# Sharing the first sequence's products with the decays between VectorE and GpSimd

## The chip, the cores and the metric

The kernel runs on one core of one Trainium2 chip. The metric is the device time of one execution in microseconds (us), the median of several runs. The core's engines are named as the profile names them: PE (TensorE, matmuls; PEld is its weight load), DVE (VectorE), ACT (ScalarE), POOL (GpSimd), and SP, which here only issues transfers. A row of the profile that ends in q (SPq, ACTq) is the issuing of a transfer.

## The reference, cut to what matters

Four sequences of 768 tokens and 8 heads go through a state-space recurrence in chunks; the result, 3072 tokens of 256 values, goes through a two-layer network with a tanh GELU between the layers.

```python
# attention-like part, for each batch and head, chunk by chunk
cum = np.cumsum(log(clip(a, 1e-6, 1)))
M = einsum('bhin,bhjn->bhij', C, B) * exp(cum_i - cum_j) * causal
y = einsum('bhij,bhjd->bhid', M, x) + einsum('bhin,bhnd->bhid', C, state) * exp(cum)
state = exp(cum_last) * state + sum_j B_j x_j exp(cum_last - cum_j)
# network
h = y.reshape(3072, 256) @ w_in            # 256 -> 2048
out = gelu_tanh(h) @ w_out                 # 2048 -> 256
```

The kernel does not form the matrix of decays. It multiplies B by a running product of decays and C by that product's reciprocal, so that the product of the two carries the ratio. These are "the products of B and C with the decays".

## The kernel before, in words

The 3072 tokens are 24 chunks of 128. The chunks are grouped in 13 units: chunk 0, chunk 1, then pairs. Sequence 0 holds the units 0 to 3 (two of one chunk, two pairs), and its preparation is written apart from that of the others, since everything waits for it.

Preparation of sequence 0. Four small loads bring the decays `a`; DVE clips them (`f_clip`, L505), forms the running product from the back (`f_R`, L509) and transposes it (`f_RT`, L513). B and C of sequence 0 arrive as 128 partitions of 6 tokens x 8 heads x 16 values. `f_mul(0)` multiplies B by the decays and `f_mul(1)` multiplies C by their reciprocal (`f_recip`, L516); both stand at L593, each is one DVE instruction over 768 elements a partition. `f_pe` (L578, L579) and the matmul `f_pp` with `f_pend` make the decay over a whole chunk. PE transposes B's product (`f_T(0,0)`, six matmuls, one for each of the six tokens, into the bank yb) and C's (`f_T(1,0)` and `f_T(1,1)`, three tokens each, into two banks hp). `f_E` copies B's bank to `bh`, and `f_F` copies C's banks to `ce` with a mask for even and one for odd heads: for each of the two banks, each of the two masks, and two stretches of columns (0 to 43, which holds the first two chunks, and 43 to 128, the rest), eight instructions. In the kernel before bank 0's first stretch is copied by ACT and bank 1's by DVE. `f_N` and `f_bn` make B's untransposed copy.

Per unit. `f_G` (L683) forms C times B in the four banks gb, `f_M` (L693) masks it causally on DVE, `f_D` (L704) forms the chunk's part of the state, `f_S` and `f_SP` (L753, L760) carry the state on DVE, `f_Y` (L726, L735) sums the output in bank yb, and `f_yev` evicts it to `xm`. From unit 4 on, `f_YDG(u)` issues Y of unit u, D and G of unit u+1 in one run. The network follows: `f_s1(u, i)` (L780) is one step of the first layer into a bank hp (there are two such banks), `f_gelu` (L788) evicts it on ACT, `f_s2(u, chunk, quarter)` (L800) adds a quarter of the second layer into o_ps or yb, `f_oev` evicts it and `f_store` stores it. `f_s1(0, i)` and `f_s1(1, i)` need the quarter i of the first weight, `f_s2(.., q)` the quarter q of the second. These weights arrive as fp32 on SP's queue during the first 23 us, and are cast to bf16 by `f_wi` (quarter, half) and `f_wo` (quarter, half), on whichever of POOL, ACT and DVE the table says. `f_castx` casts x.

Sequences 1 to 3 are prepared by other functions, all on DVE: `f_clipg`, `f_scang`, `f_rT`, `f_qT`, `f_mulg` (L552), `f_Tg` (a 32x32 transpose, L562) and `f_Fg` (the masks, L572). `f_bq` copies B's product for the `f_bn` loads.

What sets the order. Every instruction group is a node with an engine, a duration that the author estimated, its dependences and a priority. `run_order` (L39) plays the nodes through once when the kernel is built and takes, on the engine that is free first, the ready node of lowest priority; on DVE and POOL it may also leave the engine idle for a node that is due soon. The order so found is what each engine executes; the chip follows it with semaphores, engine by engine, in order. The table `PRIO` (L96 to L258) overrides the priority of every node, and `ENG` (L260) the engine of some. Where the plan has PE idle before the first step of the second layer, `idle` (L1141) puts matmuls on zeros (L1149) in its place; there are 102.

Nodes take and free buffers: two banks hp, one bank yb, one o_ps, one set gb, six o_sb.

Of the kernel before, what the change touches and what calls it, by code (L numbers as in the profile page):

```python
# [31 lines left out]
def run_order(nodes, pools, hop=0.08, same=0.04, idle=None, wait=()):  # L32
# [64 lines left out]
    'load_x(0,)': 4, 'f_par()': -99.836, 'f_hq()': -99.485, 'load_wi(0,)': 5, 'f_pari()': -101.601,  # L97
    'f_clip()': -101.591, 'load_x(1,)': 6, 'f_R()': -4.443, 'f_selq()': -64.105, 'f_RT()': -101.591,
# [172 lines left out]
def kernel(  # L271
# [10 lines left out]
    nc = tc.nc  # L282

    batch, H, S, D = x.shape
# [902 lines left out]
```

## Time and profile before

| what | value |
|---|---|
| three runs | 116.16, 115.05, 116.52 us; median 116.16 |
| the profiled execution's own time | 116.01 us |
| its span in the trace | 114.3 us (1.71 us lie around it) |
| granted PE clock | 1.00 in every stretch |
| PE busy | 108.3 us, 95% |
| DVE, ACT, POOL busy | 73.6, 72.2, 19.3 us |
| PE busy from 0 to 12.32 us (mostly matmuls on zeros) | 10.18 us |
| PE busy from 12.32 to 20 us | 7.12 of 7.68 us |
| PE busy from 20 to 30.25 us | 9.73 of 10.25 us |
| PE busy from 30.25 to 112 us | 81.26 of 81.75 us |
| DMA engines' busy share in those four stretches | 0.88, 1.08, 0.93, 0.39 |

Times in the text are counted from the start of the span. A row of the timeline gives the start, the busy time, engine, line, operation, output and inputs with their shapes, and how often it came; in brackets is how long the engine had been idle before and what ended that. Matmuls overlap: four of 256 columns take a slot of 0.44 us in the chain although their row shows 0.60.

### The profile page before, as it was taken

To read this page: it belongs to the slowest core of one execution; us is meant where nothing else is said; L and a number is where in the kernel's file an instruction comes from. 1 tells how busy PE (TensorE), PEld (TensorE's weight loads), DVE (VectorE), ACT (ScalarE), POOL (GpSimd) and SP (SyncE) were. 2 spreads that over 40 slices of the span, in tenths; PEclk is the share of its full clock that TensorE was granted. 3 is DMA by queue.
4 is the path that set the end of the run, shared out by engine and by line. 5 is a ranking of instruction groups with operands and counts; after the bars stand their busy time and mean duration, and the time that the engine had idled before them with its cause. 6 is when DMAs were issued, how large, how long until landed. Compare 5 with 4: busy or idle time off the path is not lost.

```text
span 114.3 us, 3546 instructions
## 1 busy us (share of the span) xinstructions
PE 108.3 (95%) x1466; PEld 95.7 (84%) x1466; DVE 73.6 (64%) x168; ACT 72.2 (63%) x137; POOL 19.3 (17%) x45
## 2 busy tenths in 40 slices
PE   5989898999899999999999999999999999999990
PEld 5967784988687989998988899979898889999990
DVE  5799859857997899975959899336592940000111
ACT  0537885678485467667766767675776666777710
POOL 6725536623202001202000200004000000000000
PEclk9999999999999999999999999999999999999999
DMA  1999999899376487386677102573101110111021
GB/s 44 259 325 321 380 308 256 256 206 158 103 154 120 119 192 156 101 164 125 148 186 157 51 2 69 125 148 53 49 9 46 52 46 0 46 52 46 16 73 49
DMA packets 44268, 14.77 MB, mean 129 GB/s; under 512 B 39004, under 2 KB 42716, under 8 KB 44252
## 3 DMA queue, kind: packets, MB, share of 16 engines
q1 hardware_dynamic: 43100, 14.10, 51.1%
q10 hardware_dynamic: 1152, 0.45, 1.5%
q8 instruction: 11, 0.18, 0.7%
q14 instruction: 5, 0.04, 0.1%
HBM read 10.81 MB, written 3.15 MB: 122 GB/s over the span
## 4 chain that ended last, share of the span: by engine, by line
PE 71%; DMA 13%; SPq 10%; DVE 2%; issue 1%; POOL 1%; DVEq 0%
PE hp L780 31%; PE o_ps L800 28%; DMA wf<-in_moe_w_out_dram 7%; DMA bct<-in_C_dram 4%; SPq L484 4%; PE yb L800 3%; SPq L374 3%; PE gb L683 3%; PE yb L726 2%; PE yb L735 2%; DMA a_t<-in_a_dram 2%; SPq L356 2%; PE hp L816 2%; DVE ce L572 1%; SPq L487 1%
## 5 line engine op out<-in xcount | busy, mean ns | idle before, releaser
L788 ACT ACTIVATE gT<-hp 128x512 bf16<-128x512 f32 x96 | 53.7, 596 | 24.6 <-PE hp L780 24.1
L780 PE MATMUL hp<-xm,w_in_sb 128*128 128x256 bf16 (+1 forms) x416 | 52.6, 265 | 0.5 <-ACT xm L491 0.5
L800 PE MATMUL o_ps<-w_out_sb,gT 128*128 128x256 bf16 x336 | 45.8, 273 | 0.6 <-DVE w_out_sb L495 0.6
L780 PEld LDWEIGHTS <-w_in_sb 128*128 128x128 bf16 x416 | 42.0, 114 | 3.2 <-issue 2.2
L800 PEld LDWEIGHTS <-gT 128*128 128x128 bf16 x368 | 35.3, 98 | 5.2 <-issue 0.8
L693 DVE TENSOR_TENSOR m<-gb,tri 128x1024 bf16<-128x1024 f32 (+1 forms) x25 | 28.9, 1171 | 0.0
L495 DVE COPY o_sb<-o_ps 128x256 f32<-128x256 f32 x8 | 3.4, 423 | 18.0 <-PE o_ps L800 18.0
L1149 PE MATMUL o_ps<-wz 128*128 128x128 bf16 x102 | 9.6, 260 | 1.3 <-DVE warm L394 1.3
L760 DVE SCALAR_TENSOR_TENSOR sp_new<-s_new,pend,bmask 128x256 bf16<-128x256 f32 x20 | 9.8, 500 | 0.2
L1149 PEld LDWEIGHTS <-wz 128*128 128x128 bf16 x102 | 8.2, 121 | 1.5 <-DVE warm L394 1.3
L753 DVE SCALAR_TENSOR_TENSOR s_new<-s_new,pend,hp 128x64 f32<-128x64 f32 x16 | 4.4, 277 | 5.8 <-PE hp L704 3.9
L491 ACT ACTIVATE xm<-yb 128x512 bf16<-128x512 f32 (+1 forms) x12 | 6.7, 559 | 1.0 <-PE hp L704 0.9
L491 ACT ACTIVATE o_sb<-o_ps 128x256 f32<-128x256 f32 x13 | 5.0, 386 | 3.0 <-PE o_ps L800 1.9
L735 PE MATMUL yb<-m,x 128*32 128x128 bf16 x192 | 6.4, 220 | 0.0
L493 POOL CAST x<-wf 128x512 bf16<-128x512 f32 x3 | 2.0, 682 | 25.0 <-PE hp L780 24.4
L683 PE MATMUL gb<-ce,bh 32*128 32x256 bf16 x96 | 4.9, 273 | 0.5 <-DVE ce L572 0.5
L726 PE MATMUL yb<-ce,sp_new 128*32 128x128 bf16 x160 | 5.3, 221 | 0.0
L493 POOL CAST x<-xs 128x512 bf16<-128x512 f32 x4 | 2.7, 668 | 12.9 <-DMA xs<-in_x_dram 8.6
L735 PEld LDWEIGHTS <-x 128*32 128x32 bf16 x192 | 3.8, 97 | 0.7 <-issue 0.6
L493 POOL CAST w_in_sb<-wf 128x512 bf16<-128x512 f32 x5 | 3.5, 712 | 4.5 <-DMA wf<-in_moe_w_in_dram 4.5
L726 PEld LDWEIGHTS <-sp_new 128*32 128x32 bf16 x160 | 2.9, 96 | 1.6 <-issue 1.4
L800 PE MATMUL yb<-w_out_sb,gT 128*128 128x256 bf16 x32 | 4.0, 273 | 0.0
(78 smaller groups left out, 66.7 us busy)
## 6 DMA issues: line engine op xcount, KB each, us to landing
out_dram<-o_sb SPq DMA_DIRECT2D x23, 128.0 KB, 2.1
wf<-in_moe_w_in_dram SPq DMA_DIRECT2D x4, 512.0 KB, 5.9
wf<-in_moe_w_out_dram SPq DMA_DIRECT2D x4, 512.0 KB, 7.9
xs<-in_x_dram SPq DMA_DIRECT2D x12, 128.0 KB, 3.1
xe<-in_x_dram SPq DMA_DIRECT2D x6, 128.0 KB, 6.0
bct<-in_B_dram SPq DMA_DIRECT2D x8, 96.0 KB, 4.1
bct<-in_C_dram SPq DMA_DIRECT2D x8, 96.0 KB, 2.5
wf<-in_x_dram SPq DMA_DIRECT2D x6, 128.0 KB, 3.8
```

What stands on the lines that cost most here:

```text
L484: nc.sync.dma_start(out=wfs[:, q].rearrange("p (k f) -> p k f", k=2), in_=wi[:, :, q * 512:(q + 1) * 512])
L491: nc.scalar.activation(o, i, AF.Copy)
L493: nc.gpsimd.tensor_copy(out=o, in_=i)
L683: nc.tensor.matmul(out=gb[:, g, 256 * k:256 * k + 256], lhsT=bh_of(gc)[32 * g:32 * g + 32], rhs=ce_of(gc)[32 * g:32 * g + 32], start=True, ...
L693: nc.vector.tensor_tensor(out=MT[gc][:, g0:g1], in0=gb[:, g0:g1, 256 * k:256 * k + 256] .rearrange("p g (e t) -> p g e t", e=2), in1=tri_b ...
L726: nc.tensor.matmul(out=y4[32 * j:32 * j + 32, k, w], lhsT=sp[:, 32 * h:32 * h + 32], rhs=ce_of(gc)[:, h % 2], start=first(j), stop=False, ...
L735: nc.tensor.matmul(out=y4[32 * j:32 * j + 32, k, w], lhsT=X16[u][:, k, 32 * h:32 * h + 32], rhs=m[:, h // 2, h % 2, :], start=first(j), st ...
L760: nc.vector.scalar_tensor_tensor(out=sp_new.rearrange("p (g d) -> p g d", g=4), in0=state[("s", gc)].rearrange("p (o d) -> p o d", o=1).to ...
L780: nc.tensor.matmul(out=hp[:, j * nt:(j + 1) * nt], lhsT=w_in5[:, kc, fi // 4, fi % 4], rhs=xm[:, kc, t0:t0 + nt], start=(kc == 0), stop=(k ...
L788: nc.scalar.activation(gts[v][:, i * per:(i + 1) * per, 0:nt], hps.pop((v, i)).rearrange("p (j t) -> p j t", j=per), AF.Gelu_apprx_tanh)
L800: nc.tensor.matmul(out=ops[gc], lhsT=gts[v][:, fi, tt * Q:(tt + 1) * Q], rhs=w_out_sb[:, fi, :], start=(fi == 0 and gc != 1), stop=(fi == ...
L1149: nc.tensor.matmul(out=zb[:, 0:128], lhsT=wz[:, 0:128], rhs=wz[:, 0:128], start=True, stop=True)
```

## The change

Each of the two products is split by tokens. Tokens 0 to 3 of six are multiplied on DVE, tokens 4 and 5 on POOL. `f_T(0,0)` waits for both parts of B. Of C's two transposes, the first (tokens 0 to 2) waits for DVE's part alone, the second (tokens 3 to 5) for both. The engines that copy C's banks are exchanged: bank 0's first stretch is copied by DVE, bank 1's by ACT.

```diff
-    def f_mul(i):
-        nc.vector.tensor_tensor(
-            out=bc16_of(0, i).rearrange("p (r h n) -> p r h n", r=R6, h=H),
-            in0=U[0]["bc"].rearrange("p i h (r n) -> p i r h n", r=R6)[:, i],
-            in1=(rT6[:, :, 0:H], pt)[i].rearrange("p r (h o) -> p r h o", o=1).to_broadcast([128, R6, H, N]),
+    def f_mul(i, r0, r1, eng):
+        (nc.vector if eng == "DVE" else nc.gpsimd).tensor_tensor(
+            out=bc16_of(0, i).rearrange("p (r h n) -> p r h n", r=R6, h=H)[:, r0:r1],
+            in0=U[0]["bc"].rearrange("p i h (r n) -> p i r h n", r=R6)[:, i, r0:r1],
+            in1=(rT6[:, :, 0:H], pt)[i][:, r0:r1].rearrange("p r (h o) -> p r h o", o=1)
+            .to_broadcast([128, r1 - r0, H, N]),
             op=ALU.mult)
...
-    mul_b = add("DVE", 0.97, f_mul, 0, deps=[bl[(0, 0)], RTa], prio=-82)
+
+    def muls(i, deps, prio):
+        return [add("DVE", 0.68, f_mul, i, 0, 4, "DVE", deps=deps, prio=prio),
+                add("POOL", 0.82, f_mul, i, 4, R6, "POOL", deps=deps, prio=prio)]
+
+    mul_b = muls(0, [bl[(0, 0)], RTa], -82)
     rc1 = add("DVE", 0.46, f_recip, deps=[RTa], prio=-81)
-    mul_c = add("DVE", 0.97, f_mul, 1, deps=[bl[(0, 1)], rc1], prio=-80)
+    mul_c = muls(1, [bl[(0, 1)], rc1], -80)
...
-        t0 = add("PE", 0.55, f_T, 0, 0, deps=[mul_b], prio=-87)
-        t1 = [add("PE", 0.28, f_T, 1, h, deps=[mul_c, t0], prio=-86 + 0.1 * h) for h in range(2)]
+        t0 = add("PE", 0.55, f_T, 0, 0, deps=mul_b, prio=-87)
+        t1 = [add("PE", 0.28, f_T, 1, h, deps=mul_c[:1 + h] + [t0], prio=-86 + 0.1 * h) for h in range(2)]
...
-        for h, eng in ((0, "ACT"), (1, "DVE")):
+        for h, eng in ((0, "DVE"), (1, "ACT")):
```

With it come a new `PRIO` and a new `ENG` table, so the order of nearly everything else is set anew. Read from the two built programs, engine by engine, up to the first step of unit 4:

```
DVE before: mul B, recip, mul C, pe, F x4 (bank 1), M(0) x2, S(0), SP(0), S(1), M(1), SP(1), wi(3,1), M(2), wo(0,0), M(2), ...
DVE after:  mul B, pe, recip, mul C, E(rest), F x3 (bank 0), M(0) x2, wi(1,1), S(0), SP(0), S(1), M(1), SP(1), wi(3,0), M(2) x2, ...
POOL before: castx(0), wi(0,0), wi(0,1), castx(1), wi(1,1), wi(2,0), wi(3,0), wo(0,1), castx(2), wo(1,0), wo(2,0), wo(2,1), castx(3), wo(3,1)
POOL after:  mul B, mul C, castx(0), wi(0,0), wi(0,1), wi(1,0), wi(2,0), wi(2,1), wi(3,1), wo(0,0), castx(2), wo(1,0), wo(2,0), wo(2,1), wo(3,1)
ACT before: E x2, F x2 (bank 0), bn, F x2 (bank 0), pend, wi(1,0), yev(0), wi(2,1), gelu(0,0), gelu(0,1), yev(1), ...
ACT after:  E(first), pend, F x2 (bank 1), bn, F (bank 0), castx(1), F x2 (bank 1), yev(0), gelu(0,0), gelu(0,1), gelu(0,2), yev(1), wo(0,1), ...
PE before: T(0,0), T(1,1), T(1,0), N, G(0), pp, D(0), D(1), Y(0), G(1), s1(0,0), s1(0,1), Y(1), s1(0,2), G(2), s1(1,0), s1(1,1), s1(1,2), s1(0,3), s2(0,0,0), D(2), s2(1,0,0), G(3), s1(1,3), Y(2), ...
PE after:  T(0,0), pp, T(1,0), T(1,1), N, G(0), D(0), Y(0), G(1), D(1), s1(0,0), s1(0,1), s1(0,2), Y(1), G(2), s1(0,3), s1(1,0), s2(0,0,0), s1(1,1), D(2), s2(1,0,0), G(3), s1(1,2), Y(2), s1(1,3), ...
```

Later, G(4) comes one step of the first layer later in PE's order: `f_s1(3,1)` now stands ahead of it. On DVE one transpose of B of sequence 1, `f_Tg(1,0,0,3)`, which came before C's product, now stands between C's product and C's transpose. On SP's queue the order is the same up to the second load of x of sequence 1, where the store of chunk 0 now comes first. The last 32 steps of PE are the same in both. Both kernels have 1466 matmuls, 102 of them on zeros.

More of the change, by code (lines that the diff above doesn't have):

```diff
@@ L96 @@
 PRIO = {
-    'load_x(0,)': 4, 'f_par()': -99.836, 'f_hq()': -99.485, 'load_wi(0,)': 5, 'f_pari()': -101.601,
-    'f_clip()': -101.591, 'load_x(1,)': 6, 'f_R()': -4.443, 'f_selq()': -64.105, 'f_RT()': -101.591,
[159 rows of a table removed]
+    'load_x(0,)': -30.327, 'f_par()': -123.135, 'f_hq()': -38.463, 'load_wi(0,)': -7.547,
+    'f_pari()': 1639.45, 'f_clip()': -139.498, 'load_x(1,)': -30.327, 'f_R()': 1933.95, 'f_selq()': 56.95,
[160 rows of a table added]
 }
 ENG = {
[6 rows of a table removed]
[7 rows of a table added]
 }
```

332 rows, old and new, of tables (ENG, PRIO) are left out of this document.

## The prediction

> **What bounds the kernel now.** I read the page first, then PE's waits, then the chain of waits, then the timeline of the first 22 us. The page says which engine to follow:
>
> ```profile
> PE 108.3 (95%) x1466; PEld 95.7 (84%) x1466; DVE 73.6 (64%) x168; ACT 72.2 (63%) x137; POOL 19.3 (17%) x45
> DMA  1999999899376487386677102573101110111021
> ```
>
> PE is busy 95%; the 16 DMA engines are full in slices 2 to 10, that is until 28.6 us, and not after. PE's waits, all there are behind the first row (its start):
>
> ```profile
> PE o_ps L800 <- DVE w_out_sb L495: 0.6, 1, 0.6
> PE gb L683 <- DVE ce L572: 0.5, 1, 0.5
> PE hp L780 <- ACT xm L491: 0.5, 1, 0.5
> PE yb L608 <- DVE bc L593: 0.4, 1, 0.4
> ```
>
> The last in time is L683's (G(4), at 30.25). The chain of waits says why it is late:
>
> ```profile
> 23.72 4.34 DMA bct<-in_C_dram
> ...
> 28.18 0.65 DVE bc L552 x2
> 28.86 0.39 DVE ch L562
> 29.27 0.94 DVE ce L572 x2
> ...
> 30.25 0.40 PE gb L683 x8
> ```
>
> C of sequence 1 lands at 28.09, behind the weights; three steps on DVE follow, then G(4). From there PE has no gap (81.26 of 81.75 us busy to 112). So the end is the start of G(4) plus the PE work behind it. What happens earlier counts only if it moves that start, and PE would reach G(4) 0.51 us before its input. The timeline of the first 22 us holds the edited instructions and what POOL and DVE do to each other:
>
> ```profile
> 5.48 0.96 DVE L593 TENSOR_TENSOR bc<-bct,rT 128x768 bf16<-128x768 f32 x1 [0.17 <-DMA bct<-in_B_dram]
> 6.83 0.96 DVE L593 TENSOR_TENSOR bc<-bct,pt 128x768 bf16<-128x768 f32 x1
> 7.29 0.76 POOL L493 CAST x<-xe 128x256 bf16<-128x256 f32 x1 [2.29 <-DMA xe<-in_x_dram]
> 7.71 0.36 DVE L578 TENSOR_TENSOR pe<-ac,r_t 128x3 f32<-128x3 f32 x1
> 9.79 0.40 POOL L493 CAST x<-xe 128x256 bf16<-128x256 f32 x1
> 15.53 0.87 POOL L493 CAST w_in_sb<-wf 128x512 bf16<-128x512 f32 x1 [2.09 <-DMA wf<-in_moe_w_in_dram]
> ```
>
> The same cast takes POOL 0.40 us alone and 0.76 when it starts inside DVE's product of C; and DVE's tiny `f_pe` takes 0.36 when it follows inside that cast, against 0.18 for its second half, which has more elements. So a DVE product of two tensors in SBUF and a POOL instruction hold each other up. The last row is the third quarter of the first weight after the one that came at 12.8: nothing that needs it runs before 15.5.
>
> **The products, step by step.** DVE's part: 512 of 768 elements. L593 takes 0.96 for 768, L552 0.365 for 192, so 1.03 ns an element and 0.17 fixed: 0.70 us, 0.26 less than before. POOL's part has no row. Casts of 256 and 512 take 0.40 and 0.61, so 0.19 fixed and 0.82 ns for each element read; 256 elements from two inputs read 512: 0.61. It is bounded from below by 0.40 (the cast of 256) and from above by 0.87 (the longest cast). I take 0.61, because that row reads as much.
>
> Does POOL's part run beside DVE's? By the rows of casts it does not, or only in part. If it runs behind: B on DVE 5.48 to 6.18, on POOL to 6.79; B's transposes start at 6.85, where they started at 6.50. `f_pe` waits for POOL, then 2 x 0.18, reciprocal 0.45: to 7.60. C on DVE to 8.30, on POOL to 8.91. The last C transpose starts at 8.97; the first one started at 7.85 before and the second 0.28 later. If it runs beside: 6.18 + 0.36 + 0.45 + 0.70 = 7.69 for DVE's part of C, and POOL's ends at 7.60, so C's transposes start near 7.75. That is the whole gain the edit can have here, 0.1 us, since `f_pe` has moved ahead of the reciprocal.
>
> [...]
>
> **On to the first s1 (serial case).** Bank 1 is now copied by ACT: last transpose 8.97, + 0.42 (as 7.85 to 8.27 before), two copies in 0.67: 10.06; G(0) 10.1 (9.13 before). M(0) in two halves: 10.6 to 11.85 (9.58 to 10.85 before). ACT then does bn 0.81 (10.06 to 10.87), a copy 0.48, castx(1) 0.37 (moved from POOL), two copies 0.96: 12.68, and only then yev(0) 0.37. The first s1 starts at 13.1, where it started at 12.32. Before, ACT held yev(0) behind wi(1,0), a cast that waited for its load (row at 11.37); that wait is gone, but five copies are in its place. DVE now has wi(1,1) (0.43) between M(0) and S(0): 12.28; S, SP and the wait for D(1) (G(1) at 12.7) to 13.4, M(1) 1.22 to 14.65; Y(1) at 15.1 (13.64 before), with s1(0,2) ahead of it on PE; G(2) 15.4 to 15.75 (14.55).
>
> **The load that absorbs it.** PE's next step is s1(0,3), which needs the quarter of the first weight that lands at 15.5: POOL's half ends at 16.40 (the row above). SP's queue is the same up to there, and full, so this doesn't move. PE reaches it at 16.05 in the serial case and about 15.1 in the other; both wait until 16.45. So the edited products change nothing behind 16.45, with 0.4 us to spare.
>
> From there in slots of PE: s1(0,3) and s1(1,0) 0.95, zeros 0.35, s2(0,0,0) at 17.75 (17.87 before, waiting for the second weight); but s1(1,1) and s1(1,2), which stood before it, are still to do. s1 0.45, D(2) 0.17, s2 0.44, G(3) 0.33, s1 0.45, Y(2) 0.56, s1(1,3) 0.44, two s2 0.87: s1(2,0) starts at 21.5 with no gap, and before there were 0.2 to 0.5 of gaps in such a stretch (buffers hp, gelu): 21.97 taken, against 21.47 before.
>
> From s1(2,0) to G(4) before: 16 steps x 0.437 + D 0.14 + Y 0.56 = 7.69, which took 8.10 to 29.57. After: one step more, s1(3,1): 8.13. 21.97 + 8.13 = 30.10; with 0.1 of the old 0.41 of gaps, 30.2. G(4)'s input: C at 28.18, + 0.65 + 0.39 + 0.94 as before is 30.21, and the transpose of B that now stands inside it adds up to 0.37 (30.62), or nothing where it only fills the time in which L572 waited on POOL's castx(4) (29.24 to 29.86; the two L572 took 0.92 there and 0.54 at 48.97). I take the middle, 30.45. It starts 0.20 later than before, and the work behind it is one step, 0.437, less. **Sum: 0.20 - 0.44 = -0.24 us.** The other moved casts lie under PE: before, POOL was busy 4.10 of 10.25 us between 20 and 30.25 and ACT 7.71. If that cover were gone, an ACT cast of 0.6 would delay one s1 by as much. The tail is the same steps; ACT's last eviction instead of DVE's costs 0.0 to 0.1 (0.39 against 0.42 for 256 columns).
>
> The profiled execution took 116.01; less 0.24 is 115.77. It stands 0.15 below the median of 116.16, so the forecast is **115.9**.
>
> **The rivals.** *Slower: POOL's product outlasts the cover.* Its excess e counts twice (B's and C's parts follow each other on POOL). Cover is 0.4 at s1(0,3), then PE reaches G(4) at 30.2 + (2e - 0.4). The end is that of before when PE arrives at 30.69, so from e = 0.45, POOL 1.06 us each. At POOL 1.4: 2 x 0.8 - 0.4 - 0.49 = +0.7, 116.9. It needs 2.2 us each to pass 2%. For it: no row of a two-input POOL step with runs of 16 elements; a POOL copy of 8 strided elements takes 0.32. Against: casts at 0.82 ns.
>
> *A new stall behind 30 us.* The tables move everything; M of unit 7 now follows an eviction on DVE that waits for PE, and YDG(7) comes three steps (1.3 us) earlier. Price 0.3 to 1.0, 116.6. Against: DVE is busy only 49.9 of 81.75 us there.
>
> *More gain.* If the loads of C come 0.5 earlier because chunk stores now interleave otherwise, G(4) starts when PE arrives, 30.2 less what gaps vanish: -0.5 to -0.9, 115.4. Against: SP's order up to C is unchanged and DMA is full.
>
> *The split does nothing* (serial, or parallel): same end as the forecast, as shown; it is part of it.
>
> **How the numbers follow.** Forecast 0.60 (its own range 115.6 to 116.3), POOL too slow 0.15, new stall 0.15, more gain 0.10. The three runs spread from 115.05 to 116.52, 1.47 us; so the range takes the cases 115.4 to 116.9 and some of that: 115.0 to 117.0. 2% is 2.3 us, about what a measurement of this kernel can tell from no change. No case but the far ends of POOL (over 2.2 us) or several stalls passes it: slower 0.04, faster 0.03, same 0.93.
>
> **What would show it.** In the profile after: POOL's two products at 0.6 each, starting as DVE's end; first s1 near 13.1; s1(0,3) at 16.4 to 16.6; G(4) at 30.2 to 30.7 with a short wait; no PE wait behind it. Wrong if s1(0,3) starts later than 17, if C lands at another time than 28.1, or if PE has gaps behind 31.

## The result and the profile after

| | before | after |
|---|---|---|
| median of 22 runs each, same chip | 116.06 us | 116.48 us |
| from, to | 114.78, 117.08 | 115.78, 117.63 |
| profiled execution, its span | 116.01, 114.3 | 116.09, 114.4 |
| ratio | | 1.0081 [1.0053, 1.0108] |

The kernel became slower by less than 1%: within the 2% band, on the other side of "no change" than the forecast of 115.9. The ratio leaves out runs 1.5% above a kernel's fastest, which takes more of before's wider spread, so it overstates the difference; the plain medians differ by 0.42 us. In two further sets of runs of the change, on other chips (below), its plain median lies 1.03 and 0.80 above that of before.

The page of the profile after, busy times and DMA's slices:

```profile
PE 108.5 (95%) x1466; PEld 95.6 (84%) x1466; DVE 74.3 (65%) x166; ACT 72.9 (64%) x139; POOL 20.5 (18%) x47
DMA  1999999999286487386488103760101110111021
```

POOL is busy 1.2 us more, DVE and ACT 0.7 each, PE 0.2. PE's waits behind its start have changed:

```profile
PE o_ps L803 <- POOL w_out_sb L495: 0.8, 1, 0.8
PE yb L611 <- DVE bc L595: 0.4, 1, 0.4
PE hp L611 <- DVE bc L595: 0.3, 1, 0.3
```

The wait of G(4) for C (0.5 us at L683 before) is gone. The chain shows what stands in its place, between two landings of weights:

```profile
7.51 6.79 DMA wf<-in_moe_w_in_dram
...
14.35 0.87 POOL w_in_sb L495
...
17.22 6.31 DMA wf<-in_moe_w_out_dram
...
23.58 0.88 POOL w_out_sb L495
...
24.50 0.38 PE o_ps L803 x2
...
30.88 0.33 PE gb L686 x8
```

C is not in this chain any more. The last quarter of the second weight lands at 23.53, half of it is cast by POOL in 0.88, and from there PE works without a gap to G(4) at 30.82. Before, G(4) came at 30.25 and its input decided. The timeline of the same execution, around the products:

```profile
5.35 0.69 DVE L595 TENSOR_TENSOR bc<-bct,rT 128x512 bf16<-128x512 f32 x1
5.41 1.12 POOL L595 TENSOR_TENSOR bc<-bct,rT 128x256 bf16<-128x256 f32 x1 [0.40 <-DVE rT L515]
5.96 0.58 DVE L580 TENSOR_TENSOR pe<-ac,r_t 128x3 f32<-128x3 f32 x1
6.10 0.76 PE L611 MATMUL yb<-ident,bc 128*128 128x128 bf16 x6 [0.44 <-DVE bc L595]
6.58 0.11 PEld L611 LDWEIGHTS <-bc 128*128 128x128 bf16 x2 [0.25 <-POOL bc L595]
7.23 0.69 DVE L595 TENSOR_TENSOR bc<-bct,pt 128x512 bf16<-128x512 f32 x1
7.27 1.13 POOL L595 TENSOR_TENSOR bc<-bct,pt 128x256 bf16<-128x256 f32 x1 [0.75 <-DVE pt L518]
```

DVE's part takes 0.69 (0.70 was forecast). POOL's takes 1.12 and ends 0.49 after DVE's (6.53 against 6.04). The tiny `f_pe`, behind POOL's part, takes 0.58 (0.36 before). PE did not wait for both parts: four transposes start at 6.10 and only the two of POOL's tokens wait, to 6.58. And around the first weight's last quarter and G(4):

```profile
14.32 0.43 DVE L497 CAST w_in_sb<-wf 128x512 bf16<-128x512 f32 x1
15.12 1.19 PE L783 MATMUL hp<-xm,w_in_sb 128*128 128x128 bf16 x16
...
17.48 0.60 PE L803 MATMUL o_ps<-w_out_sb,gT 128*128 128x256 bf16 x4 [0.84 <-POOL w_out_sb L495]
...
22.01 1.04 PE L783 MATMUL hp<-xm,w_in_sb 128*128 128x256 bf16 x8
...
30.82 0.40 PE L686 MATMUL gb<-ce,bh 32*128 32x256 bf16 x8
```

That quarter landed at 14.3 here, 1.2 us earlier than in the profile before. This favours the change, and still s1(2,0) starts at 22.01, later than before (21.47). From G(4) to the last pair of steps (`f_s2h`, which does the last chunk's second layer in two halves) it is 78.86 us (30.82 to 109.68), and 79.31 before (30.25 to 109.56): the one step less is there as forecast, 0.45 where 0.44 was expected. So the change gains 0.44 behind G(4) and loses more than that ahead of it.

### The profile page after: what moved, and what is told of

The parts are those of the page before. It is cut to its first block, busy times and chain, and to the rows that moved or that the text cites. A ratio compares the mean times of both kernels' runs of the same rounds, so it can differ in the third digit from the quotient of the medians.

```text
span 114.4 us, 3550 instructions
## 1 busy us (share of the span) xinstructions
PE 108.5 (95%) x1466; PEld 95.6 (84%) x1466; DVE 74.3 (65%) x166; ACT 72.9 (64%) x139; POOL 20.5 (18%) x47
## 4 chain that ended last, share of the span: by engine, by line
PE 74%; DMA 13%; issue 4%; SPq 4%; POOL 2%; ACT 0%; POOLq 0%
PE hp L783 34%; PE o_ps L803 30%; DMA wf<-in_moe_w_in_dram 6%; DMA wf<-in_moe_w_out_dram 6%; PE gb L686 3%; SPq L486 3%; PE yb L729 2%; PE yb L738 2%; PE yb L803 2%; DMA a_t<-in_a_dram 2%; SPq L358 1%; POOL w_out_sb L495 1%; POOL w_in_sb L495 1%; PE hp L707 0%; ACT o_sb L493 0%
## 5 line engine op out<-in xcount | busy, mean ns | idle before, releaser
L497 DVE COPY o_sb<-yb 128x256 f32<-128x256 f32 x2 | 0.9, 426 | 13.8 <-PE yb L803 13.8
L493 ACT ACTIVATE o_sb<-o_ps 128x256 f32<-128x256 f32 x16 | 6.2, 387 | 5.1 <-PE o_ps L803 3.0
L495 POOL COPY bq<-bc 128x384 bf16<-128x384 bf16 x5 | 2.5, 525 | 23.0 <-DVE bc L554 23.0
L574 DVE TENSOR_SCALAR ce<-ch,pari 128x192 int32<-128x192 int32 x12 | 3.6, 346 | 2.5 <-PE gb L686 2.4
L495 POOL CAST w_out_sb<-wf 128x512 bf16<-128x512 f32 x5 | 3.3, 666 | 5.4 <-DMA wf<-in_moe_w_out_dram 5.4
```

The costliest lines, as they stand in the source:

```text
L493: nc.scalar.activation(o, i, AF.Copy)
L495: nc.gpsimd.tensor_copy(out=o, in_=i)
```

## The experiments

Theory A: the new order of the steps costs the time. Theory B: the split and POOL cost it. In the diffs of orders a line is what the engine executes, in order. All medians are of 12 runs but where said; before's medians on the same chips were 115.77 to 116.02.

**Split and order apart.** The new order with undivided products, and the old order with divided ones:

```diff
 def f_mul(i, r0, r1, eng):
+    if eng == "POOL":
+        return
+    r1 = R6
```

> The changed kernel with both products undivided on DVE again (POOL's part is issued nowhere), all else in the changed order. Theory A (the time is lost between 13 and 24.5 us by the new order, around the cast wo(0,1) that now heads ACT's queue, and not by the products): first s1 moves by up to 0.4 us (12.1 to 12.5), s1(0,3) stays where its weight lands, median within 0.2 us of the changed kernel. Theory B (POOL's product of 1.12 us costs the time): G(0) earlier than 9.5, and 0.3 to 0.5 us faster than the changed kernel, back at the kernel before.

```diff
-    nc.vector.tensor_tensor(... all six tokens ...)
+    for r0, r1, eng in ((0, 4, nc.vector), (4, R6, nc.gpsimd)):
+        eng.tensor_tensor(... tokens r0 to r1 ...)
```

> The kernel before with nothing but the split: tokens 0 to 3 on DVE, 4 and 5 on POOL; order, sides and tables as before. Theory A: within 0.2 us of the kernel before, since s1(0,3) waits for its weight in any case. Theory B: 0.3 to 0.5 us slower than the kernel before, as the changed kernel is.

Measured: 116.64 (ratio 1.0085 [1.0042, 1.0128]) for the undivided products in the new order, as slow as the change; 115.50 (0.9991 [0.9955, 1.0027]) for the split in the old order. The change itself, beside them:

> The changed kernel once more, on this chip and beside the others. Both theories: 0.3 to 0.9 us slower than the kernel before. If the difference is only where loads happen to land: between 0.5 faster and 0.5 slower, and its profile shows the third weight quarter landing at another time than 14.3 us.

It took 116.80 (1.0085 [1.0048, 1.0121]). So theory B falls: the split alone neither costs nor gains, though POOL's products take 1.11 and 1.13 there too. The order costs it.

**Where in the order?** The profile after shows two places: the wait of 0.84 ahead of s2(0,0,0), and the half of the last weight that s2(0,0,3) waits for. Three kernels moved steps there:

```diff
 # e3: steps ahead of s2(0,0,0)
-ACT: yev(1), wo(0,1), gelu(0,3), gelu(1,0), gelu(1,1), wo(1,1), gelu(1,2)
+ACT: yev(1), gelu(0,3), gelu(1,0), wo(0,1), gelu(1,1), gelu(1,2), wo(1,1)
-PE: s1(1,0), zeros x6, s2(0,0,0), s1(1,1), D(2), s2(1,0,0), G(3), s1(1,2)
+PE: s1(1,0), s1(1,1), s1(1,2), s2(0,0,0), D(2), s2(1,0,0), G(3)
 # e5: a step ahead of the last weight
-PE: D(3), s2(0,0,3), s1(2,2)
+PE: D(3), s1(2,2), s2(0,0,3)
-DVE: clipg(1), scang(1), S(3,0)
+DVE: S(3,0), clipg(1), scang(1)
 # e6: both, and Tg(1,0,0,3) ahead of C's first product on DVE
```

> The changed kernel with ACT's gelu(0,3) and gelu(1,0) ahead of wo(0,1), gelu(1,2) ahead of wo(1,1), and on PE s1(1,1) and s1(1,2) ahead of s2(0,0,0), whose six matmuls on zeros are left out. Theory A: PE no longer idles 0.84 us before s2(0,0,0); s1(2,0) starts 0.5 to 0.8 us earlier than 22.0; of this 0.2 to 0.6 reaches G(4) (30.8 in the changed kernel), the rest is lost at s2(0,0,3), which waits for POOL's half of the last weight (24.45); median 0.2 to 0.6 us below the changed kernel. Theory B: no change, since the products are as they were.

> The changed kernel with s1(2,2) ahead of s2(0,0,3) on PE, the first step that reads the last weight quarter, and S(3,0) ahead of clipg(1) on DVE. In four profiles of the changed order G(4) started 7.26 to 7.29 us after that quarter landed. Theory A2 (the new order hangs the end on that landing): G(4) 6.8 to 6.9 us after the landing, median 0.3 to 0.5 us below the changed kernel. Rival R2 (the loads themselves land later in the new order, and nothing else): distance and median as in the changed kernel, within 0.15 us.

> The former and the steps-ahead version together (gelu(0,3), gelu(1,0) ahead of wo(0,1), s1(1,1) and s1(1,2) ahead of s2(0,0,0)), and the transpose of B of sequence 1 ahead of C's product. Theory A2: PE is 0.5 us or more ahead before the last weight lands, so one more wait for it can be filled only by s1(2,2); G(4) 6.6 to 6.9 us after the landing or at its own input, whichever is later; median 0.4 to 0.7 us below the changed kernel, near the kernel before. Rival R2: 0.0 to 0.2 us.

Measured: e3 116.25 (1.0057 [1.0014, 1.0100]), e5 116.33 (1.0024 [0.9991, 1.0057]), e6 116.40 (1.0042 [1.0007, 1.0078]). Each lies a little under the change and above before; none settles it. The profiled execution of e5 took 274 us, and nothing is read from it. In e3 the cast wo(0,1) came to stand behind two evictions on ACT, ran at 18.24 instead of 17.10 (the change on that chip), and held s2(0,0,0) until 18.85: the repair brought its own wait.

Two more stood beside them: the step that the change puts ahead of G(4), put there in the kernel before, and the kernel before against itself.

```diff
-PE: s1(3,0), ..., G(4), s1(3,1)
+PE: s1(3,0), ..., s1(3,1), G(4)
```

> The kernel before with s1(3,1) ahead of G(4), as the changed kernel has it, and nothing else. G(4) waited 0.51 us for its input there. If C of sequence 1 sets the start of G(4) in most executions: the step fills the wait, the end comes 0.44 us earlier from the same start, median 0.3 to 0.45 us below the kernel before. If PE is the later one in most executions: no change, within 0.1 us.

> The kernel before once more: no difference to itself (within 0.2%), and a further profile of where its loads land. Theory A2: G(4) is not at a fixed distance from the last weight's landing (7.2 and 7.2 us in the two profiles so far); if the loads alone are to blame (R2), the last weight lands 0.5 us or more before the median of the changed order's (23.5, 24.2, 22.9, 24.2).

Measured: 116.22 (1.0018 [0.9985, 1.0052]) and 115.77 (0.9977 [0.9942, 1.0013]). The step ahead of G(4) gains nothing by itself. By the author's reading it fills a wait for C where there is one (0.51 in the profile before), and delays G(4) by its own slot of 0.44 where there is none.

**The loads as the cause.** The traces showed B's loads of sequence 1 issued 0.9 us earlier in the new order, among the packets of the last weight (531 packets of 256 bytes started before its last one had ended, 231 in before). Four kernels tested that: B's loads held back; the last quarter of the second weight not loaded at all, in both orders (its casts read the third quarter again, so the output is computed with three quarters of that weight); and that quarter loaded ahead of a chunk of x.

```diff
 # e10
 def load_a(b):
+    if b == 1:
+        nc.gpsimd.memset(at[1][:, 0:1], 0.0)   # behind POOL's wo(1,0)
 # e11 (new order), e12 (old order)
 def load_wo(q):
+    if q == 3:
+        return
 # e13
-SP: load_wo(2), load_x(5), load_wo(3), load_a(1)
+SP: load_wo(2), load_wo(3), load_x(5), load_a(1)
```

> The changed kernel, in which the loads of a, B and C of sequence 1 are issued from about 19.3 us, as in the kernel before (19.3 to 19.4 there, 18.4 to 18.6 in the change), because a one-element POOL step behind the second quarter's cast writes the tile first. Theory of the loads: the small packets of B run among those of the last weight and delay it, so that it lands 3.0 to 4.0 us behind the third quarter of the second weight (2.0 to 3.3 in the old order); held back, that gap is 2.0 to 3.0 and the time falls by 0.4 to 0.8 us, to 115.7 to 116.1. Theory of the order: PE's own order between the last weight and G(4) costs the time, and nothing changes, 116.4 to 116.8. Slower than that, 117, if C's later landing takes G(4) along.

> The changed kernel without the load of the last quarter of the second weight; its casts read the third quarter again, so the output is computed with three quarters of that weight. To be read against the kernel before with the same left out. Theory of the loads: without the landing of the last weight the new order is faster than the old one by 0.2 to 0.45 us (its step less behind G(4)). Theory of the order: the new order is slower still, by 0.3 to 0.7 us.

> The kernel before without the load of the last quarter of the second weight; its casts read the third quarter again, so the output is computed with three quarters of that weight. Both theories: 0.5 to 2 us faster than before, as C lands up to 2 us earlier and PE reaches G(4) without that wait. It is the base for the changed kernel with the same left out.

> The changed kernel with the load of the last quarter of the second weight issued ahead of that of the sixth chunk of x on the same queue, and nothing else. Theory of the loads: the last weight lands some 0.5 us earlier and the end comes as much earlier: 115.7 to 116.1. Theory of the order: unchanged, 116.4 to 116.8.

Measured: e10 116.33 (1.0051 [1.0012, 1.0089]); e11 116.24 (1.0035 [0.9998, 1.0072]); e12 115.63 (0.9975 [0.9937, 1.0013]); e13 115.96 (1.0022 [0.9985, 1.0059]). Two of these four settle little. e10 issued the loads 0.6 us later (19.07 instead of 18.44), but 750 of those packets still started before the last weight's last one had ended, more than the 531. e13's median lies where the theory of the loads had it (115.7 to 116.1), and its interval holds both theories. e12 gained 0.39 by the medians, less than the 0.5 expected. The pair of e11 and e12 tells more. The loads alone are not the cause: with the last weight out of both, the new order is still 0.61 us slower (95% by resampling the runs: 0.13 to 1.00). And this pair shows what the new order costs, as the quarter of the first weight landed at nearly the same time in both. The old order (e12), timeline:

```profile
15.07 0.64 PE L782 MATMUL hp<-xm,w_in_sb 128*128 128x128 bf16 x8
15.53 0.43 DVE L497 CAST w_in_sb<-wf 128x512 bf16<-128x512 f32 x1 [1.70 <-DMA wf<-in_moe_w_in_dram]
...
15.60 0.61 PE L782 MATMUL hp<-xm,w_in_sb 128*128 128x128 bf16 x8
16.39 0.61 PE L782 MATMUL hp<-xm,w_in_sb 128*128 128x128 bf16 x8
16.89 0.61 PE L782 MATMUL hp<-xm,w_in_sb 128*128 128x128 bf16 x8
...
17.89 0.61 PE L802 MATMUL o_ps<-w_out_sb,gT 128*128 128x256 bf16 x4 [0.39 <-DVE w_out_sb L497]
...
21.50 1.04 PE L782 MATMUL hp<-xm,w_in_sb 128*128 128x256 bf16 x8
...
29.84 0.40 PE L685 MATMUL gb<-ce,bh 32*128 32x256 bf16 x8
```

The new order (e11), timeline:

```profile
15.37 0.43 DVE L499 CAST w_in_sb<-wf 128x512 bf16<-128x512 f32 x1 [1.57 <-DMA wf<-in_moe_w_in_dram]
...
15.86 0.25 PE L785 MATMUL hp<-xm,w_in_sb 128*128 128x128 bf16 x1 [0.64 <-DVE w_in_sb L499]
16.33 1.03 PE L785 MATMUL hp<-xm,w_in_sb 128*128 128x128 bf16 x15 [0.23 <-POOL w_in_sb L497]
...
17.76 0.61 PE L805 MATMUL o_ps<-w_out_sb,gT 128*128 128x256 bf16 x4
18.21 0.61 PE L785 MATMUL hp<-xm,w_in_sb 128*128 128x128 bf16 x8
...
22.27 1.04 PE L785 MATMUL hp<-xm,w_in_sb 128*128 128x256 bf16 x8
...
30.75 0.40 PE L688 MATMUL gb<-ce,bh 32*128 32x256 bf16 x8
```

In the old order PE does s1(1,0) to s1(1,2) at 15.07, 15.60 and 16.39, while the quarter lands and is cast; only s1(0,3) (16.89) is behind it. In the new order s1(0,3) heads PE's queue, PE waits for the cast (0.64 and 0.23), and the three others come behind it, two even behind s2(0,0,0). From the cast to s1(2,0) it is 5.97 in the old order and 6.90 in the new; to G(4) 14.31 and 15.38. That is 1.07 more, of which 0.44 comes back behind G(4): 0.63, and 0.61 was measured.

**Two bounds.** With e11's constant, 15.36 to 15.38, and the 7.27 that the profile after shows from the last weight's cast to G(4), G(4) in the new order is the later of two times. w is the start of the cast of the first weight's last quarter, v that of the last weight:

| execution | w | w + 15.36 | v | v + 7.27 | G(4) |
|---|---|---|---|---|---|
| the change | 14.32 | 29.68 | 23.55 | 30.82 | 30.82 |
| undivided (e1) | 14.57 | 29.93 | 22.89 | 30.16 | 30.16 |
| later loads (e10) | 14.84 | 30.20 | 23.28 | 30.55 | 30.54 |
| the change, second | 15.76 | 31.12 | 24.25 | 31.52 | 31.51 |
| last weight sooner (e13) | 16.26 | 31.62 | 22.62 | 29.89 | 31.62 |
| the change, third | 15.37 | 30.73 | 23.09 | 30.36 | 30.74 |

The last row was forecast before it ran; the others gave the rule. In the first row PE was held by a third landing as well, that of the second weight's first quarter (17.48); from there its own way gives 30.47, still under the last weight's bound. Then one stretch of the order was exchanged between the kernels (in e14 and e16 wo(0,0) and wo(0,1) also go to DVE and POOL), and e16 added two moves from above:

```diff
 # e14: the change with the old order of one stretch
-PE: G(2), zeros, s1(0,3), s1(1,0), zeros, s2(0,0,0), s1(1,1), D(2), s2(1,0,0), G(3), s1(1,2), Y(2), s1(1,3)
+PE: G(2), s1(1,0), s1(1,1), s1(1,2), s1(0,3), s2(0,0,0), D(2), s2(1,0,0), G(3), s1(1,3), Y(2)
 # e15: before with the new order of that stretch
-PE: G(2), s1(1,0), s1(1,1), s1(1,2), s1(0,3), s2(0,0,0), D(2), s2(1,0,0), G(3), s1(1,3), Y(2)
+PE: G(2), s1(0,3), s1(1,0), s2(0,0,0), s1(1,1), D(2), s2(1,0,0), G(3), s1(1,2), Y(2), s1(1,3)
 # e16: e14, with e5's moves and e13's load
```

> The changed kernel with the old order in one stretch: s1(1,0), s1(1,1) and s1(1,2) stand ahead of s1(0,3), the step that waits for the first weight's last quarter, and the first quarter of the second weight is cast by DVE and POOL instead of POOL and ACT. Theory of the steps behind the landing: s1(2,0) follows the cast of that quarter by 6.0 to 6.3 us (6.4 plus 0.5 in the change, 5.9 to 6.0 in the old order); what then binds is the last weight's landing plus 7.27, and the time falls by 0.2 to 0.6 us against the change, to 115.9 to 116.2. Rival, the cost lies between the last weight and G(4): s1(2,0) is earlier but the time stays, 116.4 to 116.8.

> The kernel before with the new order in one stretch: s1(0,3) ahead of s1(1,0), s1(1,1) and s1(1,2), the last two behind s2(0,0,0). Theory of the steps behind the landing: s1(2,0) follows the cast of the first weight's last quarter by 6.9 us instead of 5.95, and G(4) by 15.2 instead of 14.3; where C or the last weight bound it, part of that is covered. Time 116.3 to 117.0, 0.3 to 0.9 above before. Rival: unchanged, 115.9 to 116.1.

> The changed kernel with three moves at once: the old order of the steps around s1(0,3), s1(2,2) ahead of the last quarter's first product with chunk 0's step (as in the run that put the step before the last weight), and the last weight's load ahead of the sixth chunk of x. Theory of the steps behind the landing: no bound of the old order is later any more and the one step behind G(4) is saved, so 0.3 to 0.5 us under before: 115.4 to 115.8. Rival: as the change, 116.2 or more.

> The changed kernel itself, on the same chip as the three others: 116.3 to 116.8. In its profile G(4) is at the later of two times: the cast of the first weight's last quarter plus 15.36 us, and the cast of the last weight's quarter plus 7.27 us.

Measured: e14 116.65 (1.0060 [1.0019, 1.0102]); e15 116.68 (1.0069 [1.0036, 1.0102]); e16 117.07 (6 runs; 1.0114 [1.0058, 1.0170]); the change 116.65 (1.0065 [1.0031, 1.0098]). In e15 Y(2) also came to stand ahead of a step that updates the state it reads, so part of its output is computed from an older state. e15 makes before as slow as the change. With 23.04, s1(2,0) came 7.5 behind the cast, more than the 6.9 expected: PE waits 0.62 just before it for an eviction on ACT, which the edit brought with it. So e15 may overstate what the steps behind the landing cost. e14 came out as the rival had it. Its timeline:

```profile
21.52 1.04 PE L785 MATMUL hp<-xm,w_in_sb 128*128 128x256 bf16 x8
...
23.34 0.43 DVE L497 CAST w_out_sb<-wf 128x512 bf16<-128x512 f32 x1 [0.52 <-DMA wf<-in_moe_w_out_dram]
23.37 0.87 POOL L495 CAST w_out_sb<-wf 128x512 bf16<-128x512 f32 x1 [1.96 <-DMA wf<-in_moe_w_out_dram]
...
23.82 0.85 PE L805 MATMUL o_ps<-w_out_sb,gT 128*128 128x256 bf16 x4 [0.25 <-DVE w_out_sb L497]
...
30.60 0.40 PE L688 MATMUL gb<-ce,bh 32*128 32x256 bf16 x8
```

s1(2,0) is at 21.52, 6.1 behind the cast, as the theory wanted; but then PE waits for the last weight (v = 23.34) and G(4) is at v + 7.26. The one bound gone, the other holds. e16 loads that weight sooner and pays elsewhere; its timeline:

```profile
23.00 0.63 ACT L493 ACTIVATE x<-xe 128x512 bf16<-128x512 f32 x1 [1.05 <-DMA bct<-in_B_dram]
23.54 1.07 ACT L793 ACTIVATE gT<-hp 128x512 bf16<-128x512 f32 x2
24.16 0.21 PE L709 MATMUL hp<-x,bn 128*32 128x64 bf16 x4 [0.62 <-ACT gT L793]
24.65 0.60 PE L785 MATMUL hp<-xm,w_in_sb 128*128 128x256 bf16 x4 [0.27 <-ACT gT L793]
```

The chunk of x that it put behind the weight holds ACT until 23.00, two evictions queue behind that cast, and PE waits 0.62 and 0.27 for them.

**Both bounds taken away.** e17 is e14 without the last weight's load (e11's edit). e18 computes everything: e14, e13's load, the cast of the late x moved from ACT to POOL behind the last weight's cast, and D(3) behind s2(0,0,3).

```diff
 # e18, beside e14's and e13's edits
-ACT: gelu(1,3), castx(3), gelu(2,0)        POOL: wo(2,1), wo(3,1)
+ACT: gelu(1,3), gelu(2,0)                  POOL: wo(2,1), wo(3,1), castx(3)
-PE: s2(0,0,2), D(3), s2(0,0,3), s1(2,2)
+PE: s2(0,0,2), s2(0,0,3), D(3), s1(2,2)
```

> The changed kernel with the steps around s1(0,3) in the old order and without the load of the last weight's last quarter, whose casts read the third quarter again, so the output is computed with three quarters of that weight. Each of the two was done alone before, and each alone left the time at 116.2 to 116.7. Theory of two bounds, of which G(4) takes the later (first weight's last quarter plus 15.36, last weight plus 7.27): with both gone G(4) comes near 30.0 and the time is 115.1 to 115.6, 0.3 to 0.8 under before. Rival, something else in the new order holds it up: 116.2 or more.

> The full computation, with both bounds moved: the changed kernel with the steps around s1(0,3) in the old order, the last weight's load ahead of that of the sixth chunk of x, the cast of that x on POOL behind the last weight's cast instead of on ACT, and D(3) one step later on PE. Theory of two bounds: the last weight lands near 21.7, G(4) at 30.0 to 30.5, time 115.2 to 115.8, 0.1 to 0.7 under before. Rival: 116.2 or more; or a new wait for the later x at D(3), 0.3 to 0.6 of it.

Measured: e17 115.42 (0.9966 [0.9937, 0.9995]), e18 115.68 (0.9993 [0.9964, 1.0021]), before 115.93. Alone, the two edits of e17 had left the time at 116.65 and 116.24; together they bring it 0.8 us below the better of the two. The timeline of e17:

```profile
15.20 1.05 PE L787 MATMUL hp<-xm,w_in_sb 128*128 128x128 bf16 x16 [0.29 <-ACT xm L495]
15.49 0.43 DVE L499 CAST w_in_sb<-wf 128x512 bf16<-128x512 f32 x1 [1.61 <-DMA wf<-in_moe_w_in_dram]
...
17.69 0.61 PE L807 MATMUL o_ps<-w_out_sb,gT 128*128 128x256 bf16 x4
...
21.29 1.04 PE L787 MATMUL hp<-xm,w_in_sb 128*128 128x256 bf16 x8
...
29.77 0.40 PE L690 MATMUL gb<-ce,bh 32*128 32x256 bf16 x8
```

PE works through the landing, and G(4) comes at 29.77. So in the new order these two bounds set the start of G(4), and with both gone the loss is gone. e18 has G(4) at 30.30; it is faster than the change (the intervals of their ratios to before do not meet) and not told from before.

The two bounds do not share the loss alike, for the old order waits for the last weight too. The timeline of before's second execution:

```profile
24.23 0.63 ACT L491 ACTIVATE w_out_sb<-wf 128x512 bf16<-128x512 f32 x1 [0.56 <-DMA wf<-in_moe_w_out_dram]
...
24.91 0.60 PE L800 MATMUL o_ps<-w_out_sb,gT 128*128 128x256 bf16 x4 [0.35 <-ACT w_out_sb L491]
...
31.05 0.40 PE L683 MATMUL gb<-ce,bh 32*128 32x256 bf16 x8
```

G(4) comes 6.82 behind that cast here, and 7.16 behind it in e2 (24.21, 31.37). In the new order it is 7.27, and 0.44 of it comes back behind G(4), which leaves 6.83. So the bound of the last weight is no higher in the new order and explains no loss by itself. The one that rose is the first: 15.38 less 0.44 is 14.94, where the old order has 14.31. This leaves e14 in part unexplained. Its first bound is near the old one, and its profile, with 116.18, is 0.17 above that of before, yet its plain median is 0.79 above. About 0.3 of that lies behind G(4), from where the profiled execution takes 85.58 to its end and the change's three take 85.27 to 85.31; no run shows what the rest is.

## Why the prediction was wrong, step by step

- *The place that decides, and the step behind it.* Right: the end is fixed from G(4), and one step less behind it is worth 0.45 (79.31 to 78.86).
- *The products.* DVE's 0.69 was right (0.70). POOL's row shows 1.12, above the upper bound of 0.87, but it starts with DVE's, so it can hold a wait for it; behind DVE's end it takes 0.49, where the serial case had 0.61. `f_pe` behind it takes 0.58. The serial case was the author's estimate from the casts' 0.40 and 0.76. In the trace after, POOL's part, which started 0.06 behind DVE's, ends 0.49 behind its end, and the `f_pe` that DVE began at 5.96 ends with POOL's part (6.54 and 6.53).
- *On to the first s1.* Forecast 13.1, measured 12.14 (12.32 before). The transposes wait token by token and not for the whole product (6.10, and 6.58 for the last two), which the sum did not have, and yev(0) came at 11.70 instead of 12.7.
- *The load that absorbs it.* Right that the products change nothing behind it (e2). Wrong to take its 15.5 as fixed: in the traces of both kernels and of the experiments that quarter was cast from 14.3 to 16.3.
- *From s2(0,0,0) to s1(2,0): the step that failed.* "s1(2,0) starts at 21.5 with no gap" adds nine steps to 17.75 and leaves out the slot of s2(0,0,0) itself, 0.44. In e11 the way from 17.76 to 22.27 takes 4.51, where the sum had 3.71, or 4.22 with the gaps that took it to 21.97. It did note that s1(1,1) and s1(1,2) "are still to do", but it had s1(2,0) only 0.5 later than before; from the cast of the first weight's last quarter it is 0.93 later (6.90 in e11, 5.97 in e12), as in the old order three steps are done while that quarter lands.
- *From s1(2,0) to G(4): failed too.* "8.13; with 0.1 of the old 0.41 of gaps". Without any wait for a load it is 8.48 (e11 and e17, alike), so 0.35 of gaps stayed, where 0.1 was allowed.
- *What follows from these two.* Corrected, PE reaches G(4) at 17.75 + 4.51 + 8.48 = 30.74, behind its input (30.20 measured at the end of L574, 30.45 forecast). C itself came as forecast (its product starts at 28.03), but it no longer decides: 0.49 is lost and 0.44 won, with nothing left, even in an execution like before's profile. That moves the sum from -0.24 to +0.05. The wait for the last weight, which the sum does not contain, adds 0.35 in the profile after (30.82, where PE's own way from 17.48 gives 30.47), but before's second execution has such a wait of 0.35 too. What else makes the 0.42 of the medians is not shown. The measured 116.48 lies inside the stated range of 115.0 to 117.0, but not by the mechanism: the range was widened for the spread of the runs and for a slow POOL, and POOL was not the cause.
- *The rivals.* "POOL's product outlasts the cover" set its point at 1.06 us each, and the row shows 1.12; but first s1 came earlier, not later, and e2 shows that POOL is not the cause. "A new stall behind 30 us" did not come: PE has no gap behind G(4).
- *What stays open.* The profiled executions alone would not have shown the loss (116.09, 116.78 and 116.05 for the change; 116.01 and 116.86 for before). The landings of the timed runs are not seen. That the steps behind the first weight's landing cost the time rests on e11 with e12, and on e15 and e17; e14, which moved them alone, did not recover it. In e14 and e17, s1(6,0) came 0.26 late (54.21 in e14); its cause was not tried.

## What to carry to other kernels

When an order changes around a landing, count which steps lie behind it in each order: a step that was done during the wait was free, and behind the landing it takes time of its own (here from the cast to s1(2,0) 6.90 in e11, where e12 took 5.97). Add such a sum against a row whose answer is known, the old order first; that would have shown the missing slot. And where one edit that removes a bound changes nothing, look for a second bound of nearly the same height before the theory is given up: here each of two repairs alone showed nothing, and both together 0.8 us. Then take the height of that second bound in the old version as well: here it was as high there, so it can hide a repair without having made the loss.

## What the runs showed of the hardware

- What came by the same load, at the same place of the queue, was cast up to 1.4 and 1.9 us later in one execution than in another: the last weight from 22.89 (e1) to 24.25 (the change, second), the first weight's last quarter from 14.32 (the change) to 16.26 (e13).
- A POOL product of 256 elements took 1.12 and 1.13 us in the change and 1.11 and 1.13 in e2, beside a DVE product of 512 that took 0.69 in both.
- The last weight's two casts took 0.43 on DVE and 0.87 on POOL together in the profile after (23.55 and 23.58), and 0.63 on ACT and 0.61 on POOL in before (both from 23.08): POOL's took 0.26 longer there beside DVE's than beside ACT's. Where POOL's cast started first, in before at 16.92, it took 0.61 and DVE's, from 16.98, 0.83.
